# Layer 1 of a fused attention and expert kernel: seven half products for eight on the last 768 tokens of four weight pairs

## Chip, cores and metric

The kernel runs on one NeuronCore of a Trainium2 chip. The metric is the device time of one execution in microseconds (us). Names of engines: PE is TensorE (matmul) and PEld its weight loads, DVE is VectorE, ACT is ScalarE, POOL is GpSimd, SP is the engine that issues most DMAs (SPq in the rows).

## Reference: what is computed

Sigmoid attention over 4 batches, 12 heads, 448 positions of 64, then two layers on the 1792 tokens of 768 features. Layer 1 takes the maximum of three products; its 768x768 weights come as float64 and are converted to float32 on the chip. Layer 2 multiplies by `w_out`; then each token goes to one of 8 experts.

```python
scores = scale * np.matmul(q, k.transpose(0, 1, 3, 2)) - np.log(S)
attn = 1.0 / (1.0 + np.exp(-scores))
x = np.matmul(attn, v)                      # then as (1792, 768)
h = np.maximum(np.maximum(x @ w1, x @ w2), x @ w3)
x = h @ w_out
logits = x @ w_gate + modality_bias[modality_id]
e_idx = np.argmax(logits, axis=1)           # one expert of 8 per token
out[mask] = gate_w[mask, None] * (np.maximum(x[mask] @ w1[e], 0.0) @ w2[e])
```

## The kernel before

Every float32 product is made from two parts of each operand, a rounded high part and the rest (`split`, L184: ACT or DVE writes the high part, DVE the rest), with three matmuls per 128x128 block: high times high, high times low, low times high.

**Stages on PE, in order of time:** attention (L318, L334, L344, L352), layer 1 (`project`, L499), layer 2 in two passes (`layer2`, L563), the experts (L900, L916, L928). PE, DVE, ACT and SP run their instructions in the order in which the code emits them; each engine waits at the head of its queue, and so does SP with its DMAs.

**Layer 1.** Six blocks of 128 output features (`fb`), in each two halves of the tokens (1024, then 768), in each the three weights (`wi`). One call of `project` is a *step* of 36 matmuls: 6 blocks of input features, 3 matmuls each, on two halves of the step's tokens (2x512 or 2x384 columns). It accumulates in one of two PSUM tiles `acc` that take turns. At its end ACT copies the result into `hT` (L503, first weight) or DVE takes the maximum (L505, second and third). `hA` (tag H1) and `hB` (H2) hold all six blocks of h until layer 2.

**Weights.** A *chunk* is one float64 block of 768x128 weights (768 KB) or 128 rows of `w_out`. SP loads it into one of two `stage` buffers, six DVE operations (`cv_ops`, L164) convert it, and `split` puts the parts into one of four places of `w_ring`. All of that, and the products of `w_out` with the gate (`gate_op`, L480, 48 of them), stands in a queue `bg`/`bg2`, from which `background` takes operations after each step until an estimate of their cost is used up (6.6 or 4.8).

**End of layer 1.** While the last steps run, `split_a` and `split_h` make the operands of the first two token tiles of layer 2; `pass_a` then takes the 14 tiles of 128 tokens in order.

Of the kernel before, what the change touches and what calls it, by code (L numbers as in the profile page):

```python
# [23 lines left out]
E64_LO = float(np.uint32(0x38000000).view(np.float32))  # L24
E64_HI = float(np.uint32(0x47EFFFFF).view(np.float32))


@with_exitstack
def attn_moe_kernel(
# [136 lines left out]
    def cv_ops(i, dst):  # L166
# [206 lines left out]
    with tc.manual_schedule(engines={mybir.EngineType.PE, mybir.EngineType.Activation, mybir.EngineType.DVE, SP}):  # L373
# [46 lines left out]
        for j in range(NU // 2 + 1):  # L420
# [48 lines left out]
        gk = hold("K1", "gk", 3 * DM)  # L469
        wgb = [cut(gk, DM * i, DM) for i in range(2)]  # L470
        junk = cut(gk, 2 * DM, DM)

        def gate_load(e):
            for i, (op, cost, at) in enumerate(bg2):
                if at == 1000 + e:
                    bg2[i] = (op, cost, step[0] + 1)
            nc.sync.dma_start(out=wgb[e % 2], in_=wgT[e].partition_broadcast(128))

        def gate_op(e, kb):
            nc.vector.scalar_tensor_tensor(out=junk, in0=wof[kb], scalar=1.0, in1=wgb[e % 2], op0=ALU.mult,  # L480
                                           op1=ALU.mult, accum_out=gw[:, kb, e:e + 1])
# [6 lines left out]

        def project(fb, half, wi):
            while (fb, wi) not in ready:  # L490
                background(0.1, late=0)
            m = w_ring[ring_no[fb, wi]]
            acc = ps_a([128, 2, 512], "acc")
            c0 = HALF * half
            cw = (min(c0 + HALF, NT) - c0) // 2
# [5 lines left out]
            dst = hT[fb][:, c0:c0 + 2 * cw].rearrange("p (c s) -> p c s", c=2)  # L501
            if wi == 0:
                nc.scalar.activation(out=dst, in_=acc[:, :, 0:cw], func=ACTF.Copy)  # L503
            else:
                nc.vector.tensor_tensor(out=dst, in0=dst, in1=acc[:, :, 0:cw], op=ALU.max)  # L505
            if half == 1:
                used[fb, wi] = step[0]

        CA = 256
# [3 lines left out]
        def hs_view(a):  # L515
            return a.rearrange("p (a k c) -> p a k c", a=2, k=KB)

        def split_h(t, hs):
            for h_, k0, k1 in ((hA, 0, 4), (hB, 4, 6)):
                src = h_[:, :, 128 * t:128 * (t + 1)]  # L520
                split(hs[:, 0, k0:k1], hs[:, 1, k0:k1], src)
# [6 lines left out]

        for fb in range(KB):
            for half in range(2):  # L530
                for wi in range(3):
                    project(fb, half, wi)
                    step[0] += 1
                    background(6.6 if half == 0 else 4.8)
                    if fb == KB - 1 and half == 1:

                        assert not bg and not bg2
                        for i in ((0,), (1, 2), ())[wi]:
                            split_a(i)
                        if wi < 2:  # L540
                            hs1[wi] = hs_view(w_ring_[1][:, 0] if wi == 0 else hold("K1", "hs_k", 2 * DM))
                            split_h(wi, hs1[wi])


        wo_ck = hold("P2a", "wo_ck", 2 * KB * DM)
# [24 lines left out]
        def end_a(t):  # L570
            acc = acc_t.pop(t)
            nc.scalar.activation(out=xoa[t % 2], in_=acc[:, 0:CA], func=ACTF.Copy)
            nc.vector.tensor_tensor(out=lg[:, t], in0=bias_t[:, t], in1=acc[:, CA:NA], op=ALU.add)
            nc.sync.dma_start(out=x2d[0][128 * t:128 * (t + 1), 0:CA], in_=xoa[t % 2])

# [448 lines left out]
        def end_b(p, c=None):  # L1024
            rows = slice(128 * toks[p], 128 * (toks[p] + 1))
            a, b = out_b(p, c)
# [8 lines left out]
        def put_gate(p):  # L1035
            b = out_b(p, None if p < P0 else 1)[1]
            nc.vector.tensor_copy(out=b[:, DM - 512:DM - 511], in_=gate[:, toks[p]:toks[p] + 1])

# [221 lines left out]
```

## Time and profile before

| what | value |
|---|---|
| median of 3 runs | 735.28 us (734.99 to 736.02) |
| the profiled execution | 731.45 us, of which the span shown in the trace is 729.6 us |
| PE busy | 721.0 us, 99% of the span |
| DVE, ACT, POOL busy | 486.5, 263.2, 77.0 us |
| layer 1 on PE | 131.74 to 391.53 us |
[...]

Busy PE counts pipelined matmuls, so it says that PE has no pauses, not that it is at its peak. The other engines work beside PE; their time counts only where PE waits for them.

### The profile page before, as it was taken

How to read it: one execution, taken by the hardware profiler on the slowest of the kernel's cores; microseconds unless marked ns; L12 is line 12 of the kernel's file. 1: busy time of each engine (PE TensorE's matmuls, PEld its weight loads, DVE VectorE, ACT ScalarE, POOL GpSimd, SP SyncE). 2: the span in 40 equal slices, each digit the busy share in tenths (PEclk: the TensorE clock that was granted, in tenths of full speed). 3: DMA queues.
4: the chain of work that ended last, by engine and by line, in shares of the span. 5: the costliest groups of instructions: out<-in, count | busy, mean ns of one | idle time of the engine just before them, and what ended most of it. 6: DMA issues, size and time to landing. Idle time of an engine off the chain costs nothing.

```text
span 729.6 us, 10665 instructions
## 1 busy us (share of the span) xinstructions
PE 721.0 (99%) x4164; PEld 613.9 (84%) x4164; DVE 486.5 (67%) x845; ACT 263.2 (36%) x410; POOL 77.0 (11%) x96
## 2 busy tenths in 40 slices
PE   8999999999999999999999999999999999999996
PEld 5455545799898988989899988998998899999996
DVE  4677885666877879873125657146895698689363
ACT  5665566000011010100123533243661474375352
POOL 3000000000000000000001004453025005101101
PEclk9999999999999999999999999999999999999999
DMA  8856761141332321310000113668154025515101
GB/s 204 214 158 167 195 185 54 44 130 54 124 129 91 95 94 44 108 44 1 0 1 22 66 53 126 191 190 308 57 190 158 0 75 174 199 53 193 51 2 63
DMA packets 42330, 78.58 MB, mean 108 GB/s; under 512 B 6201, under 2 KB 28794, under 8 KB 42276
## 3 DMA queue, kind: packets, MB, share of 16 engines
q1 hardware_dynamic: 38420, 66.10, 30.0%
q0 software_dynamic: 3776, 11.63, 4.6%
q8 instruction: 35, 0.57, 0.3%
q14 instruction: 19, 0.16, 0.1%
q10 hardware_dynamic: 80, 0.11, 0.1%
HBM read 69.79 MB, written 11.58 MB: 112 GB/s over the span
## 4 chain that ended last, share of the span: by engine, by line
PE 98%; DMA 0%; SPq 0%; issue 0%; DVE 0%; POOL 0%; POOLq 0%; ACT 0%; ACTq 0%
PE acc L499 36%; PE hacc L900 16%; PE oacc L928 12%; PE X L344 8%; PE s L318 7%; PE acc_b L563 5%; PE acc_a L563 4%; PE oacc L916 3%; PE acc_c L563 3%; PE X L352 2%; PE xT L788 1%; PE s L334 1%; DMA u<-in_qk_dram 0%; SPq L269 0%; PE wgp L360 0%
## 5 line engine op out<-in xcount | busy, mean ns | idle before, releaser
L499 PE MATMUL acc<-xR,w_ring 128*128 128x512 f32 (+1 forms) x864 | 208.3, 362 | 0.0
L499 PEld LDWEIGHTS acc<-xR,w_ring 128*128 128x128 f32 x864 | 157.6, 188 | 17.6 <-issue 0.7
L900 PE MATMUL hacc<-xh,wo_ck 128*128 128x512 f32 (+3 forms) x600 | 120.6, 361 | 0.0
L900 PEld LDWEIGHTS hacc<-xh,wo_ck 128*128 128x128 f32 x600 | 107.1, 188 | 12.1 <-DVE xo L948 0.3
L499 PE MATMUL acc<-xLa,w_ring 128*128 128x512 f32 (+1 forms) x360 | 101.3, 362 | 0.0
L301 ACT ACTIVATE at<-s,nlns 128x896 f32<-128x896 f32 x84 | 77.9, 1007 | 44.4 <-PE s L318 43.0
L928 PE MATMUL oacc<-wo_ck,hx 128*128 128x384 f32 x504 | 90.3, 336 | 0.0
L928 PEld LDWEIGHTS oacc<-wo_ck,hx 128*128 128x128 f32 x504 | 87.2, 188 | 0.2
L189 DVE TENSOR_TENSOR wo_ck<-raw,wo_ck 128x512 fp32r<-128x512 f32 (+1 forms) x87 | 68.4, 807 | 24.6 <-ACT wo_ck L188 24.5
L499 PEld LDWEIGHTS acc<-xLa,w_ring 128*128 128x128 f32 x360 | 66.3, 188 | 7.1
L188 ACT ACTIVATE wo_ck<-raw 128x512 fp32r<-128x512 f32 (+1 forms) x87 | 59.6, 723 | 18.6 <-DVE raw L823 7.6
L318 PEld LDWEIGHTS s<-kq 64*128 64x128 f32 x432 | 37.9, 185 | 21.3 <-issue 15.5
L318 PE MATMUL s<-kq 64*128 64x448 f32 x432 | 50.9, 376 | 0.8 <-ACT kq L287 0.8
L503 ACT ACTIVATE hA<-acc 128x1024 f32<-128x1024 f32 (+1 forms) x8 | 7.4, 922 | 118.3 <-PE acc L499 118.3
L480 DVE SCALAR_TENSOR_TENSOR gk<-wof,gk 128x768 f32<-128x768 f32 x48 | 45.9, 957 | 1.4
L997 POOL MEMSET xo<- 128x544 f32 x5 | 2.6, 550 | 410.6 <-PE acc_a L563 382.1
L775 POOL DMA_INDIRECT xg<-x2d,idx x30 | 36.5, 1218 | 74.1 <-PE xT L788 43.8
L344 PE MATMUL X<-at,u 128*64 128x448 f32 x192 | 37.8, 543 | 0.0
L370 DVE CAST xR<-X 128x448 fp32r<-128x448 f32 x24 | 14.9, 619 | 31.9 <-PE X L352 31.9
L505 DVE TENSOR_TENSOR hB<-hB,acc 128x1024 f32<-128x1024 f32 (+1 forms) x8 | 8.7, 1088 | 39.5 <-PE acc L499 39.4
L188 ACT ACTIVATE w_ring<-cv 128x768 fp32r<-128x768 f32 x14 | 11.8, 842 | 54.7 <-PE acc L499 54.7
L505 DVE TENSOR_TENSOR hA<-hA,acc 128x1024 f32<-128x1024 f32 (+1 forms) x16 | 17.4, 1087 | 20.3 <-PE acc L499 19.9
(260 smaller groups left out, 885.2 us busy)
## 6 DMA issues: line engine op xcount, KB each, us to landing
stage<-in_moe_w_dram SPq DMA_DIRECT2D x18, 768.0 KB, 4.5
raw<-in_moe_w_dram SPq DMA_DIRECT2D x12, 1024.0 KB, 5.7
u<-in_qk_dram SPq DMA_DIRECT2D x46, 224.0 KB, 4.8
raw<-in_moe_w_dram SPq DMA_DIRECT2D x12, 768.0 KB, 4.8
stage<-in_moe_w_out_dram SPq DMA_DIRECT2D x6, 768.0 KB
x2d<-xo SPq DMA_DIRECT2D x28, 128.0 KB, 1.7
gk<-wgT SPq DMA_DIRECT2D x8, 384.0 KB, 5.4
rawb<-in_moe_w_dram SPq DMA_DIRECT2D x4, 768.0 KB, 4.6
```

The source lines that it names most:

```text
L188: nc.scalar.activation(out=r(dR), in_=src, func=ACTF.Copy)
L189: nc.vector.tensor_tensor(out=r(dL), in0=src, in1=dR, op=ALU.subtract)
L301: nc.scalar.activation(out=dst, in_=s[:, :, 0:S], func=ACTF.Sigmoid, scale=qscale, bias=nlns)
L318: nc.tensor.matmul(s[g][:, h, 0:S], r(kt[p, a, 0, 128 * g:128 * (g + 1)]), r(kt[p, x, 1]), start=(n == 0), stop=(n == 2))
L344: nc.tensor.matmul(X_t[u][64 * h:64 * h + 64, 0:S], vt[:, 2 * g + h], at[:, 2 * g + h], start=(g == 0), stop=False)
L480: nc.vector.scalar_tensor_tensor(out=junk, in0=wof[kb], scalar=1.0, in1=wgb[e % 2], op0=ALU.mult, op1=ALU.mult, accum_out=gw[:, kb, e:e + 1])
L499: nc.tensor.matmul(acc[:, c, 0:cw], r(m[:, a, kk, :]), r(x[kk][:, c0 + cw * c:c0 + cw * (c + 1)]), start=(kk == 0 and n == 0), stop=(kk == ...
L505: nc.vector.tensor_tensor(out=dst, in0=dst, in1=acc[:, :, 0:cw], op=ALU.max)
L563: nc.tensor.matmul(acc, r(hs[:, a, kk, :]), r(w(kk, b)), start=(kk == 0 and n == 0), stop=(kk == KB - 1 and n == 2))
L775: d = nc.gpsimd.indirect_dma_start(out=xg[s][:, XC[c][0]:XC[c][1]], out_offset=None, in_=x2d[c], in_offset=bass.IndirectOffsetOnAxis(ap=ix ...
L900: st["mm"] = nc.tensor.matmul(acc[:, f, t0:t1], r(w[a][:, k, 128 * f:128 * (f + 1)]), r(x[:, 2 * c + k, t0:t1]), start=(t0 == 0 and c == 0 ...
L928: nc.tensor.matmul(o[:, s, 0:HC], r(hz[k][:, x, 2 * c + f, 128 * s:128 * (s + 1)]), r(w[a][:, f]), start=(first and c == 0 and f == 0 and ...
```

## The change

Layer 1 is now nine *jobs*: three pairs of feature blocks (`p`), for each the three weights. Jobs 0 to 4 are four `plain` steps as before, with the 768 tokens first (n = 0, 1 for the two blocks), then the 1024 (n = 2, 3). Jobs 5 to 8 compute the last 768 tokens of both blocks together by seven products of half-size operands (`s_block`: A11 B11, S2 T2, A12 B21, S1 T1, S3 T3, A22 T4, S4 B22), each of 9 matmuls of 384 columns, where there were two steps, that is eight such products; then two plain steps (f = 0, 1) of 1024 tokens. Sums of the tokens' operands (T1 to T4) are made once, in jobs 0 and 4; sums of the weights (S1 to S4) for each job.

With it come these:

- Conversion: ACT makes the first operation (`conv_start`), DVE four (`conv_end`) instead of six.
- From chunk 16 on (job 5's weights) all loads go into one `stage` buffer, and the next load is issued behind the conversion's last read; the other buffer (tag S1) holds the sums `sm`.
- The order of the side work is written out (`plan`, `do_tasks`, `hook`). In jobs 5 to 7 one chunk is converted in the last step, one inside `s_block` behind the first product (`hook(0)`).
- H1 holds the T sums, so h of pairs 0 and 1 is written to HBM (`spill`) and read back into `hA` in job 8.
- Layer 2 takes the tokens from 1024 on first (`tok`).

```diff
+    hd = dram.tile([128 * (KB - 2), NT], F32, name="hd")
...
+    def conv_start():
...
+        if k < NC1:
+            load_chunk()
+        v = cv1 if k >= NC1 or k % 2 == 0 else cv2
+        st = stage[k % 2 if k < NC1 else 0]
+        hf = st.bitcast(F32).rearrange("p (n two) -> p n two", two=2)[:, :, 1]
+        nc.scalar.activation(out=v, in_=hf, func=ACTF.Copy, scale=E64_SC)
+        return k, v, st
+
+    def conv_end(c, dsts):
...
+        ve.tensor_scalar(out=v, in0=v, scalar1=-E64_TOP, scalar2=E64_TOP, op0=ALU.max, op1=ALU.min)
+        ve.tensor_scalar(out=v.bitcast(I32), in0=v.bitcast(I32), scalar1=3, scalar2=None, op0=ALU.logical_shift_left)
+        ve.scalar_tensor_tensor(out=v.bitcast(U32), in0=lo.bitcast(U32), scalar=29, in1=v.bitcast(U32),
+                                op0=ALU.logical_shift_right, op1=ALU.bitwise_or)
+        for d, c0, c1 in dsts or [(v, 0, DM)]:
+            ve.scalar_tensor_tensor(out=d.bitcast(U32), in0=hi[:, c0:c1].bitcast(U32), scalar=0x80000000,
+                                    in1=v[:, c0:c1].bitcast(U32), op0=ALU.bitwise_and, op1=ALU.bitwise_or)
+        if k >= NC1:
+            load_chunk()
+        return v
...
-            nc.sync.dma_start(out=stage[i % 2].rearrange("p (a c) -> p a c", a=n), in_=src)
+            nc.sync.dma_start(out=stage[i % 2 if i < NC1 else 0].rearrange("p (a c) -> p a c", a=n), in_=src)
...
+        def s_sums():
+            ve_ = nc.vector.tensor_tensor
+            ve_(out=part(0), in0=raw_b[0], in1=raw_b[1], op=ALU.add)
+            ve_(out=part(1), in0=part(0), in1=raw_a[0], op=ALU.subtract)
+            ve_(out=part(2), in0=raw_a[0], in1=raw_b[0], op=ALU.subtract)
+            ve_(out=part(3), in0=raw_a[1], in1=part(1), op=ALU.subtract)
...
+        def prod(a, b, g, first):
+            a, b = aop(a), bop(b)
+            for kk in range(K2):
+                for n, (i, x) in enumerate(((0, 0), (0, 1), (1, 0))):
+                    nc.tensor.matmul(g[:, 0:SW], r(a(i, kk)), r(b(x, kk)), start=(first and kk == 0 and n == 0),
+                                     stop=(kk == K2 - 1 and n == 2), skip_group_check=not first)
...
+            prod("A11", "B11", g0, True)
+            nc.scalar.activation(out=t1, in_=g0[:, c], func=ACTF.Copy)
+            hook(0)
+            prod("S2", "T2", g1, True)
+            ve_(out=t2, in0=t1, in1=g1[:, c], op=ALU.add)
+            hook(1)
+            prod("A12", "B21", g0, False)
+            take(g0[:, c], hp[:, 0, S0_], wi)
+            hook(2)
+            prod("S1", "T1", g2, True)
+            hook(3)
+            prod("S3", "T3", g1, False)
+            ve_(out=t3, in0=t1, in1=g1[:, c], op=ALU.add)
+            fin(t3, g2, hp[:, 1, S1_])
...
+        plan.update({(FJ - 1, 0): "ca", (FJ - 1, 1): "cb", (FJ - 1, 2): "T3", (FJ - 1, 3): "S cn"})
...
+            split_aw(1)
+            if j == FJ:
+                s_split(1)
+
+            def hook(i):
+                step[0] += 1
+                if i == 0 and not end:
+                    conv_end(conv_start(), DST[1])
+
+            s_block(hp, wi, hook)
...
+            if end:
...
+                hA = hold("H1", "hA", 4, NT)
+                for c in (S0_, S1_, slice(0, HALF // 2), slice(HALF // 2, HALF)):
+                    nc.sync.dma_start(out=hA[:, :, c], in_=hd.rearrange("(k p) n -> p k n", p=128)[:, :, c])
...
+                elif f == 0:
+                    s_sums()
+                    for i in range(2):
+                        s_split(i)
+                    background(2.1)
+                else:
+                    background(2.1)
+                    split_aw(0)
+                    if j < NJOB - 2:
+                        conv_end(conv_start(), DST[0])
+                take(acc, hp[:, f, B0_], wi)
```

On PE, a step of 768 tokens before (one block, one weight) begins like this; its results go to `acc`, and its first matmul waits for the reader of that PSUM tile:

```order
L499 MATMUL acc<-xR,w_ring_78 128x384 [waits DVE_49]
L499 MATMUL acc<-xR,w_ring_78 128x384
L499 MATMUL acc<-xLa,w_ring_78 128x384 x2
L499 MATMUL acc<-xR,w_ring_78 128x384 x4
L499 MATMUL acc<-xLa,w_ring_78 128x384 x2
L499 MATMUL acc<-xR,w_ring_78 128x384 x4
```

In job 5 of the changed kernel, from the second product (S2 T2 into g1, here `g_2232`) to the start of the fifth (S3 T3, into the same g1), PE has this:

```order
L637 MATMUL g_2232<-tT,w_ring_78 128x384 x6
L637 MATMUL g_2231<-xR,w_ring_79 128x384 [waits Activation_49]
L637 MATMUL g_2231<-xLa,w_ring_79 128x384
L637 MATMUL g_2231<-xR,w_ring_79 128x384 x2
L637 MATMUL g_2231<-xLa,w_ring_79 128x384
L637 MATMUL g_2231<-xR,w_ring_79 128x384 x2
L637 MATMUL g_2231<-xLb,w_ring_79 128x384
L637 MATMUL g_2231<-xR,w_ring_79 128x384
L637 MATMUL g_2233<-tT,w_ring_78 128x384 x9
L637 MATMUL g_2232<-xR,w_ring_78 128x384 [waits DVE_49]
```

The fifth product adds to g1, so its first matmul waits for DVE's reading of g1 (`t2`, L657); between the two stand only the third and fourth product.

On DVE, a conversion before stands like this at one of the last steps of layer 1 (`cv` is the converted chunk); it is six operations, and a late one delays only the `take` of a step behind it (L505):

```order
L172 TENSOR_SCALAR cv<-stage_75 128x768
L173 TENSOR_SCALAR cv<-cv 128x768
L174 TENSOR_SCALAR cv<-cv 128x768
L176 SCALAR_TENSOR_TENSOR cv<-stage_75,cv 128x768
L178 TENSOR_SCALAR cv<-stage_75 128x768
L180 TENSOR_TENSOR cv<-cv 128x768
L505 TENSOR_TENSOR hA<-hA,acc 128x768
L189 TENSOR_TENSOR w_ring_79<-cv,w_ring_79 128x768
```

From the last `take` of job 4 into job 5's `s_block`, the changed kernel has this on DVE (`sm` the sums, `h_1845` h of pair 1):

```order
L631 TENSOR_TENSOR h_1845<-h_1845,acc 128x1024
L221 TENSOR_TENSOR w_ring_79<-cv,w_ring_79 128x768
L221 TENSOR_TENSOR w_ring_78<-sm,w_ring_78 128x768
L204 TENSOR_SCALAR cv<-cv 128x768
L205 TENSOR_SCALAR cv<-cv 128x768
L206 SCALAR_TENSOR_TENSOR cv<-stage_75,cv 128x768
L209 SCALAR_TENSOR_TENSOR cv<-stage_75,cv 128x768
L657 TENSOR_TENSOR sm<-sm,g_2232 128x384
L631 TENSOR_TENSOR h_1845<-h_1845,g_2231 128x384
L665 TENSOR_TENSOR sm<-sm,g_2232 128x384
```

A whole conversion (L204 to L209) now stands ahead of the reading of g1 (L657).

On SP, the last loads of layer 1 before take turns between the two buffers (`gk` are the gate's operands):

```order
L223 DMA stage_75<-in_moe_w_dram 128x6x256
L223 DMA stage_76<-in_moe_w_dram 128x6x256
L223 DMA stage_75<-in_moe_w_dram 128x6x256
L477 DMA gk<-wgT 128x768 x3
L223 DMA stage_76<-in_moe_w_dram 128x6x256
L223 DMA stage_75<-in_moe_w_dram 128x6x256
L223 DMA stage_76<-in_moe_w_dram 128x6x256
```

In the changed kernel the loads from job 4 on (chunks 17 to 23) all go into one buffer, with the spills between them and the reading back at the end:

```order
L261 DMA stage_75<-in_moe_w_dram 128x6x256 x4
L677 DMA hd<-h_1845 128x768 x2
L514 DMA gk<-wgT 128x768
L677 DMA hd<-h_1845 128x1024
L261 DMA stage_75<-in_moe_w_dram 128x6x256
L677 DMA hd<-h_1845 128x1024
L261 DMA stage_75<-in_moe_w_dram 128x6x256 x2
L772 DMA hA<-hd 128x4x384 x2
L772 DMA hA<-hd 128x4x512 x2
```

No load of chunks 17 to 23 can be issued ahead of the last reading of the chunk before it.

## Rows read from the trace of the kernel before

**Rows 1.** The page: busy time of the engines, and granted TensorE clock in 40 slices.

```profile
PE 721.0 (99%) x4164; PEld 613.9 (84%) x4164; DVE 486.5 (67%) x845; ACT 263.2 (36%) x410; POOL 77.0 (11%) x96
...
PEclk9999999999999999999999999999999999999999
```

**Rows 2.** Chain that ended last, in order of time: start us, us, what, count.

```profile
131.74 259.79 PE acc L499 x1296
391.53 30.54 PE acc_a L563 x252
...
534.66 4.17 PE oacc L928 x24
```

**Rows 3.** Who waited for whom; total us, times, longest: PE, whole span.

```profile
PE warm L391 <- DVE nlns L379: 1.3, 1, 1.3
PE s L318 <- ACT kq L287: 0.8, 1, 0.8
```

**Rows 4.** Timeline 120 to 160 us: start us, us, engine, line: last part of x.

```profile
133.62 0.62 DVE L371 TENSOR_TENSOR xLb<-X,xR 128x448 fp32r<-128x448 f32 x1
```

**Rows 5.** Groups by shape, VectorE, 131 to 395 us: count, busy us, mean ns, idle before.

```profile
L480 DVE SCALAR_TENSOR_TENSOR gk<-wof,gk 128x768 f32<-128x768 f32 x48 | 45.9, 957 | 1.4
L176 DVE SCALAR_TENSOR_TENSOR cv<-stage,cv 128x768 uint32<-128x768 uint32 x20 | 19.2, 958 | 0.7
...
L173 DVE TENSOR_SCALAR cv<-cv 128x768 f32<-128x768 f32 x20 | 11.2, 561 | 0.7
...
L505 DVE TENSOR_TENSOR hA<-hA,acc 128x1024 f32<-128x1024 f32 x8 | 9.8, 1219 | 5.2 <-PE acc L499 5.2
L505 DVE TENSOR_TENSOR hA<-hA,acc 128x768 f32<-128x768 f32 x8 | 7.6, 955 | 15.0 <-PE acc L499 14.6
...
L480 DVE DVE_READ_ACCUMULATOR gk<-wof,gk 128x1 f32 x48 | 4.0, 82 | 0.0
...
L189 DVE TENSOR_TENSOR wo_a<-wof,wo_a 128x512 fp32r<-128x512 f32 x3 | 2.1, 688 | 6.4 <-ACT wo_a L188 6.4
...
L189 DVE TENSOR_TENSOR hs_p<-hB,hs_p 128x256 fp32r<-128x256 f32 x2 | 0.8, 421 | 0.0
```

**Rows 6.** Groups by shape, ScalarE, whole span.

```profile
L188 ACT ACTIVATE w_ring<-cv 128x768 fp32r<-128x768 f32 x14 | 11.8, 842 | 54.7 <-PE acc L499 54.7
...
L188 ACT ACTIVATE hs_p<-hA 128x512 fp32r<-128x512 f32 x7 | 4.4, 623 | 8.1 <-PE acc L499 8.1
L503 ACT ACTIVATE hA<-acc 128x1024 f32<-128x1024 f32 x4 | 4.1, 1030 | 34.3 <-PE acc L499 34.3
...
L942 ACT ACTIVATE xo<-oacc,gcol 128x384 f32<-128x384 f32 x6 | 3.5, 580 | 0.3
```

**Rows 7.** Timeline 300 to 312 us, one conversion and the next load.

```profile
301.91 0.56 DVE L174 TENSOR_SCALAR cv<-cv 128x768 int32<-128x768 int32 x1
...
302.50 0.96 DVE L176 SCALAR_TENSOR_TENSOR cv<-stage,cv 128x768 uint32<-128x768 uint32 x1
...
303.38 0.56 DVE L178 TENSOR_SCALAR cv<-stage 128x768 uint32<-128x768 uint32 x1
...
303.96 6.57 SPq L223 DMA_DIRECT2D stage<-in_moe_w_dram  x2
```

**Rows 8.** DMA issues: count, KB each, median us from issue to landing.

```profile
stage<-in_moe_w_dram SPq DMA_DIRECT2D x18, 768.0 KB, 4.5
...
x2d<-xo SPq DMA_DIRECT2D x28, 128.0 KB, 1.7
```

**Rows 9.** Tile stage, 260 to 345 us: landing time of its loads.

```profile
DMA to landing us min/median/max: 4.5/5.1/5.6
```

**Rows 10.** Busy us (instructions) of PE, PEld, DVE, ACT, POOL; PEclk; DMA share; GB/s.

```profile
4.00:6.00 2.00, 1.25 (x9) 0.94 (x10) 1.58 (x4) 0.39 (x1) 2.00 (x8) 1.00 0.82 238
304.50:307.50 3.00, 3.00 (x15) 2.53 (x15) 2.85 (x4) 0.85 (x1) 0.00 (x0) 1.00 0.82 247
```

More of the change, by code (lines that the diff above doesn't have):

```diff
@@ L487, in attn_moe_kernel, with xpart @@
                 bg2.extend((lambda e=e - 1, kb=kb: gate_op(e, kb), US_SUM, 1000 + e - 1) for kb in range(KB))
[L489 to L492, printed above, removed]
+        def xpart(x, k, c):
+            if x == 0:
+                return [(slice(0, K2), xR_[:, K2 * k:K2 * (k + 1), c])]
+            if k == 0:
+                return [(slice(0, K2), xLa[:, 0:K2, c])]
+            return [(slice(0, K2 - 1), xLa[:, K2:KB - 1, c]), (slice(K2 - 1, K2), xLb[:, :, c])]
@@ new lines, in minus_plus, with step_, t_prep @@
+        def minus_plus(d, first, rest):
+            def step_(a, b, op):
+                for sl, ap in b:
+                    nc.vector.tensor_tensor(out=d[:, sl], in0=a[:, sl], in1=ap, op=op)
+            ops = [lambda: step_(*first, ALU.subtract)]
+            ops += [lambda p=p, op=op: step_(d, p, op) for op, p in rest]
+            return ops
+        US_T = 1.35
+        ADD, SUB = ALU.add, ALU.subtract
+        def t_prep():
+            tt = hold("K1", "tt", 2, K2, SW)
+            tA, tB = tt[:, 0], tt[:, 1]
+            whole = lambda a: [(slice(0, K2), a)]
+            ops = minus_plus(tA, (xpart(0, 0, S1_)[0][1], xpart(0, 0, S0_)), [(SUB, xpart(1, 0, S0_)), (ADD, xpart(1, 0, S1_))])
+            ops.append(lambda: split(tT[:, 0, 0], tT[:, 0, 1], tA))
+            ops += minus_plus(tB, (xpart(0, 1, S1_)[0][1], whole(tA)), [(ADD, xpart(1, 1, S1_))])
+            ops.append(lambda: split(tT[:, 1, 0], tT[:, 1, 1], tB))
+            ops += minus_plus(tA, (xpart(0, 1, S0_)[0][1], whole(tB)), [(ADD, xpart(1, 1, S0_))])
+            ops.append(lambda: split(tT[:, 2, 0], tT[:, 2, 1], tA))
+            return ops
@@ L493, in project, with s_split, split_aw, plain @@
+        def s_split(i):
+            m = sw_[i]
+            split(flat(m[:, 0]), flat(m[:, 1]), cut(sm_[0], 2 * QW * i, 2 * QW))
+        def split_aw(f):
+            if f:
+                split(flat(aw[1][:, 0]), flat(aw[1][:, 1]), cv2)
+                return
+            for k, src in enumerate(raw_a):
+                split(ksl(aw[0], 0, k), ksl(aw[0], 1, k), src)
+        def plain(m, c0, n_tok):
             acc = ps_a([128, 2, 512], "acc")
-            c0 = HALF * half
-            cw = (min(c0 + HALF, NT) - c0) // 2
+            cw = n_tok // 2
@@ L504, in project @@
             else:
[L505 to L507 removed]
+                nc.vector.tensor_tensor(out=dst, in0=dst, in1=acc, op=ALU.max)
+        def prod(a, b, g, first):
[4 more added lines that the diff above has]
+                                     stop=(kk == K2 - 1 and n == 2), skip_group_check=not first)
@@ new lines, in s_block, with fin @@
+        def s_block(hp, wi, hook):
+            g0, g1 = (ps(f"x{i}", [128, 512], f"g{i}") for i in range(2))
+            g2 = ps("t", [128, 2, 512], "g2")[:, 0]
+            t1, t2, t3, t4 = (part(i) for i in range(4))
+            c = slice(0, SW)
+            ve_ = nc.vector.tensor_tensor
+            def fin(u, g, dst):
+                d = dst if wi == 0 else t4
+                ve_(out=d, in0=u, in1=g[:, c], op=ALU.add)
+                if wi:
+                    ve_(out=dst, in0=dst, in1=t4, op=ALU.max)
+            prod("A11", "B11", g0, True)
[12 more added lines that the diff above has]
+            fin(t3, g2, hp[:, 1, S1_])
+            hook(4)
+            g3 = ps("x0", [128, 512], "g3")
+            prod("A22", "T4", g3, True)
+            fin(t3, g3, hp[:, 1, S0_])
+            hook(5)
+            prod("S4", "B22", g2, False)
+            fin(t2, g2, hp[:, 0, S1_])
+            hook(6)
@@ L511, in attn_moe_kernel, with spill @@
+        def spill(p, hp, f, c):
+            nc.sync.dma_start(out=hd[128 * (2 * p + f):128 * (2 * p + f + 1), c], in_=hp[:, f, c])
+        B0_, B1_ = slice(0, HALF), slice(HALF, NT)
         CA = 256
@@ L527, in split_a @@
             split(w[:, :, 0, CA:NA], w[:, :, 1, CA:NA], gw[:, 2 * i:2 * i + 2, 0:E])
[L529 to L532, printed above, removed]
-                    step[0] += 1
[L534 to L542, printed above, removed]
+        tq = deque(t_prep())
@@ L1024, in end_b @@
         def end_b(p, c=None):
-            rows = slice(128 * toks[p], 128 * (toks[p] + 1))
+            rows = slice(128 * tok[toks[p]], 128 * (tok[toks[p]] + 1))
             a, b = out_b(p, c)
```

175 lines of the change are left out of this document (142 added, 33 removed).

## Prediction

> **What bounds the kernel now.** I read the page first: PE is busy for 99% of the span, at a granted clock in the highest tenth in every slice [rows 1]. The chain that ended last is PE from one end to the other, layer 1 as one piece of 259.79 us with 1296 matmuls [rows 2]. The waits say the same: after its first instruction PE waited once, 0.8 us, and never in layer 1 [rows 3]. So PE's own work sets the time. Whatever takes matmuls away is worth their length, and whatever makes PE wait costs its whole length, since no slack lies behind. DVE and ACT have time to spare over the whole, but they work in a fixed order, and where PE needs a reading of theirs, their place in that order decides.
>
> **The gain.** 24 matmuls of 384 columns take 4.17 us [rows 2], so 0.174 us each. Layer 1 has 648 of those, 112.6 us; the other 648, of 512 columns, take the remaining 147.2, so 0.227 each. A step of 36 is then 6.26 or 8.18 us, a job of four steps 28.88, a half product of nine 1.56 and a block of seven 10.95 in place of 12.51. Four blocks save 4 x 1.56 = **6.26 us**. That the nine now write one PSUM tile without a turn costs nothing by the rows: `pass_a` does that and takes 30.54/252 = 0.121 us for 264 columns [rows 2], in proportion to the columns as 0.174 is.
>
> [...]
>
> **The prices of side work.** On DVE [rows 5]: a two-operand pass over 768 elements 0.96 us, over 512 0.69, over 256 0.42, so by these an estimate of 0.55 for 384 and 1.35 for 1152; the maximum of a step (`take`) 1.22 or 0.96; a gate product 0.96 + 0.08, which I take as 1.0. A one-operand pass is 0.56, and a dependent one follows after 0.60 [rows 7]. On ACT [rows 6]: 0.84 for 768, 0.62 for 512, 1.03 for a `take` of 1024, 0.58 for 384 from PSUM. The new conversion is then 0.84 on ACT, then 0.60 + 0.60 + 0.99 + 0.96 = 3.15 on DVE (3.2 where its last pass is in two halves). A load is issued 0.02 us after the last reading of its buffer [rows 7] and lands 4.5 us later in the median [rows 8]; in the late stretch of layer 1 it was 4.5 to 5.6 [rows 9]. No row has an ACT pass over every second element, which the conversion now begins with; I take the price of a plain one.
>
> **The new wait.** In each block the fifth product adds to g1, which DVE has to read first (`t2`, 0.55). PE reaches it after four products, 6.26 us into the block. In jobs 5, 6 and 7 a whole conversion stands ahead of `t2` on DVE, and its chunk is loaded only after the conversion before it has ended, because one buffer serves all. Both are followed here; handing over costs about 0.05 each time.
>
> *Job 5.* From job 4's start: ACT's `take` of job 3 and its conversion, 1.95; DVE 3.2, at 5.15 the load of chunk 17 goes out; landed 9.65, ACT 0.85, DVE 3.15, at 13.7. A gate product and a `take`, 15.6. T3: passes over 1152, 1152, 768 and 384, 4.2, then ACT 1.2 and DVE 1.4 for its parts, 22.4. Gate and `take`, 24.6 (PE ended that step at 20.7, so DVE is what is late). Four sums 2.1 and a split 0.9, 27.6. The conversion of chunk 18, 3.2, at 30.8: only now is chunk 19 loaded, and PE began the block at 28.88. Landing 4.5, ACT 0.85, DVE 3.15, `t2` 0.55 and the handing over 0.15 make 40.0, which is 11.1 into the block: **4.8 us of pause**.
>
> *Job 6.* From the end of job 5's first plain step: `take` 1.22, two gate products 2.0, two half splits 1.0, conversion 3.2, so the load goes out at 7.45, 0.7 before the block (the step in between is 8.18). Landed 3.8 into it; 4.65 more for ACT, DVE, `t2` and handing over, 8.45: **2.2 us**.
>
> *Job 7.* Here ACT makes the `take`s: 1.03, two copies 1.0, conversion 0.85, DVE 3.2 make 6.1, so the load goes out 2.1 before the block, lands at 2.4, and 4.65 more give 7.05: **0.8 us**. Job 8 has no conversion in its block: `take` 1.22 and a split 1.0 end before the second product does, no pause.
>
> Together **7.8 us**. With 5.6 us for each load (job 5 has two in its chain) they would be 12.2; with 4.4 and DVE's passes 5% shorter, 5.6.
>
> **What I cost at nothing, and its cover.**
> - The sums T1, T2, T4 (ten tasks in job 0) and the late start of DVE's work there: ACT makes job 0's `take`s, so DVE may run into job 1. By the same prices DVE is about 6 us behind when job 1 begins, and its `take` of that job's first step ends at 12.2 into the job, when PE is about to reuse that PSUM tile at 12.5. That cover is thin, 0.3 us; beyond it each us counts.
> - The first step now reads the last tokens of attention. DVE has written them by 134.24 us [rows 4], 2.5 us into layer 1; PE needs the fifth block of features at 24 x 0.174 = 4.2.
> - The spills (384 and 512 KB, after a `take`): nearest rows 128 KB in 1.7 us and 768 KB in 4.5 [rows 8], so between these. h of the next pair is written at the earliest 6.26 us after the last one's `take` began; on SP they stand ahead of loads, but are issued before those loads could be. If not hidden: up to 1 us each.
> - The reading back, 3.67 MB, goes out when the sixth product of job 8 has ended, 9.4 into its block. At 247 GB/s, measured while a load ran [rows 10], it lasts 15 us and ends at about 26.5. The first quarter, some 3 us and the landing time, is needed at 20; the last part from 33 on. Seven us of cover.
> - Handing over between products: no row has PE waiting on a semaphore that was given long before; 0 to 0.1 for each, I take 0.
>
> **The sum.** Against the profiled execution: 731.45 - 6.26 + 7.8 = 733.0. The median of the runs lies 3.83 above that execution (735.28), so I add the difference to it: 735.28 + 1.5 = **736.8 us**. What PE saves on products it loses at the fifth product of three blocks, to a load that starts too late. With the bounds above this case reaches from 734.6 to 741.2; I expect 735 to 739.
>
> **Rivals.**
>
> *The loads arrive in time (faster).* If DVE gets through job 4 faster than my sum, chunk 19 goes out earlier, and every us there is a us less pause. For: 27 passes and two loads stand in that chain, and an error adds up; the order leaves DVE free to run ahead. Against: DVE waits 2.3 us for chunk 17 whatever happens, and 4.8 us would be a sixth of its chain. With no pause in any job: 735.28 - 6.26 = 729.0; with half of them 732.9. It is faster by over 0.2% if the pauses make less than 4.8 together. Chance 0.19.
>
> *The clock falls (slower).* PE would stand still for 4.8 us in job 5. [...] It decides only if the pause is there at all. Chance 0.15.
> [...]
>
> *Something I cost at nothing is late (slower).* Most likely the first `take`s of job 1, or the spills and the reading back where they meet loads: 1 to 4 us on top, 738 to 741. The point is 0.3 us of delay in job 1, or the reading back at half its rate. Chance 0.08.
>
> **How the numbers follow.** The forecast has 0.58, at 736.8. Below 733.8 or above 736.75 a time differs from 735.28 by over 0.2%, about what a measurement of this kernel can tell from no change. Of the forecast's 0.58 some 0.23 lie within that; with 0.01 of the first rival that makes *same* 0.24. *Faster* is the rest of the first rival, 0.18. *Slower* is 0.35 + 0.15 + 0.08 = 0.58. For 8 in 10 the range runs from 731.5, which leaves out two thirds of the first rival, to 740.5, which leaves out the worst of the last two.
>
> **What would show it.** In the changed kernel's waits, PE should wait for DVE `sm` at L657 three times, about 4.8, 2.2 and 0.8 us, at the first matmul of S3 T3, and ACT's conversion just before for the load of `stage`. Layer 1 on PE should last about 261 us with 1260 matmuls. The granted clock after the longest pause tells the second rival. The forecast is wrong if those waits are short (then DVE's chain in job 4 is where to look), if half products are slower than 0.174 us a matmul, or if `pass_a` waits for `hA`.

## Result, and the profile after

| | median | before, same chip | ratio, 95% interval |
|---|---|---|---|
| the changed kernel | 739.03 us (736.15 to 741.59, 8 runs) | 735.08 us | 1.0052 (1.0027 to 1.0077) |
| again (e5) | 736.47 us (735.27 to 739.00, 10 runs) | 734.66 us | 1.0032 (1.0020 to 1.0044) |

It is slower, by 2 to 4 us. The forecast was 736.8, the range 731.5 to 740.5, and the rival in which the clock falls had a chance of 0.15. The profiled execution of the first row took 741.45 us, its span is 739.6; it is next to the longest of the eight.

The page of the changed kernel, the rows that answer to [rows 1]: PE is busy for 98% of the span, and one slice of the granted clock is below the highest tenth (its mean is 0.992, in the kernel before 0.999).

```profile
PE 722.7 (98%) x4128; PEld 613.2 (83%) x4128; DVE 511.4 (69%) x880; ACT 293.7 (40%) x449; POOL 77.3 (10%) x96
...
PEclk9999999999999998999999999999999999999999
```

The chain that ended last (start us, us, what, count) answers to [rows 2]. Layer 1 on PE goes from 134.49 to 399.33 us, 264.84 where it was 259.79; the forecast was about 261. The lines of 27 matmuls are what follows a wait in a block, products five to seven.

```profile
134.49 115.68 PE acc L621 x576
...
289.39 7.11 PE g L637 x27
...
320.91 6.54 PE g L637 x27
...
350.65 4.98 PE g L637 x27
...
372.00 10.97 PE g L637 x63
...
399.33 30.52 PE acc_a L816 x252
```

In the block of job 8, where nothing waits, 63 matmuls take 10.97 us (10.95 expected); so 27 take 4.70. Behind the three waits they took 7.11, 6.54 and 4.98. Behind the last the granted clock was 1.00 (350.65 to 355.63 us), so its 0.28 us more is not the clock's; below it is called the restart.

Who waited for whom (total us, times, longest), PE, whole span, answers to [rows 3]:

```profile
PE g L637 <- DVE sm L657: 6.5, 3, 4.1
PE acc_c L816 <- issue: 1.5, 2, 0.8
...
PE s L351 <- DVE kq L321: 0.9, 1, 0.9
```

The first line is the wait that was forecast. The chain to it in job 5 (start us, us, engine, line; in brackets the idle time before and what ended it):

```profile
278.86 0.33 PE L637 MATMUL g<-xR,w_ring 128*128 128x384 f32 x1
...
279.30 1.03 DVE L209 SCALAR_TENSOR_TENSOR wof<-stage,cv 128x384 uint32<-128x384 uint32 x2
...
280.24 1.21 DVE L631 TENSOR_TENSOR h<-h,acc 128x1024 f32<-128x1024 f32 x1
...
280.40 8.92 SPq L261 DMA_DIRECT2D stage<-in_moe_w_dram  x2
...
284.81 0.89 ACT L195 ACTIVATE cv<-stage 128x768 f32<-128x768 f32 x1 [3.67 <-DMA stage<-in_moe_w_dram]
285.73 0.56 DVE L204 TENSOR_SCALAR cv<-cv 128x768 f32<-128x768 f32 x1 [2.54 <-ACT cv L195]
...
287.92 0.96 DVE L209 SCALAR_TENSOR_TENSOR cv<-stage,cv 128x768 uint32<-128x768 uint32 x1
288.79 0.55 DVE L657 TENSOR_TENSOR sm<-sm,g 128x384 f32<-128x384 f32 x1
...
289.39 0.69 PE L637 MATMUL g<-xR,w_ring 128*128 128x384 f32 x1 [4.10 <-DVE sm L657]
```

The load of chunk 19 goes out at 280.40, when the conversion of chunk 18 has ended, 1.54 us after the first product of the block began (278.86). 4.4 us later ACT begins, then DVE's four passes, then `t2`, then PE, which had waited 4.10 us. The rows of jobs 6 and 7:

```profile
320.91 0.44 PE L637 MATMUL g<-xR,w_ring 128*128 128x384 f32 x1 [1.78 <-DVE sm L657]
...
350.65 0.45 PE L637 MATMUL g<-xR,w_ring 128*128 128x384 f32 x1 [0.57 <-DVE sm L657]
```

The stretches around the waits of jobs 5 and 6 (PE, PEld, DVE, ACT, POOL busy us with instructions, then PEclk, DMA share, GB/s) answer to [rows 10]:

```profile
283.00:285.00 2.00, 2.00 (x14) 1.97 (x12) 0.19 (x1) 0.19 (x1) 0.00 (x0) 1.00 0.54 192
...
287.00:289.40 2.40, 0.01 (x1) 0.01 (x1) 2.37 (x4) 0.00 (x0) 0.00 (x0) 0.55 0.00 0
289.40:291.00 1.60, 1.60 (x5) 1.60 (x6) 0.40 (x1) 0.00 (x0) 0.00 (x0) 0.50 0.33 112
...
293.50:294.60 1.10, 1.10 (x7) 1.10 (x6) 0.88 (x2) 0.00 (x0) 0.00 (x0) 0.74 0.00 0
294.60:295.00 0.40, 0.40 (x4) 0.40 (x3) 0.05 (x1) 0.00 (x0) 0.00 (x0) 1.00 0.00 0
...
318.00:320.90 2.90, 1.13 (x7) 0.81 (x5) 2.79 (x4) 0.10 (x1) 0.00 (x0) 1.00 0.00 0
320.90:322.00 1.10, 1.09 (x5) 1.09 (x6) 0.00 (x0) 0.00 (x0) 0.00 (x0) 0.72 0.20 47
322.00:324.00 2.00, 2.00 (x8) 2.00 (x7) 0.18 (x1) 0.00 (x0) 0.00 (x0) 0.50 1.03 357
```

While PE stands in job 5, the granted clock falls: its mean is 0.55 from 287.00 to 289.40; while PE works again it is 0.50 up to 293.50, 0.74 from there to 294.60, and then 1.00. In job 6 it was still 1.00 up to 320.90, while PE stood, and was at 0.50 only from 322.00 to 324.00, when PE worked again.

So layer 1 is accounted for: 253.82 without any wait (measured below), 6.45 of waiting and 4.53 of slower products behind the waits make 264.80.

Outside of layer 1 this execution was 4.9 us longer than the rows of before: 2.75 ahead of it (the first 18 products of the program began 0.8 us later and took 3.73 us, before 2.09) and 2.15 in the last pass of layer 2 (L816, 1.5 of it the waits for `issue` above). Neither comes with the change as such: of the 13 other traces one has that slow start (e6), and the `issue` waits stand in all four that were taken on one chip (e5 to e8) and in none of the eight of e1 to e4 and e9 to e12. Whether the kernel before has such waits on that chip is not shown, as it was not traced there.

### The profile page after: what moved, and what is told of

The parts are those of the page before. It is cut to its first block, busy times and chain, and to the rows that moved or that the text cites. A ratio compares the mean times of both kernels' runs of the same rounds, so it can differ in the third digit from the quotient of the medians.

```text
span 739.6 us, 10728 instructions
## 1 busy us (share of the span) xinstructions
PE 722.7 (98%) x4128; PEld 613.2 (83%) x4128; DVE 511.4 (69%) x880; ACT 293.7 (40%) x449; POOL 77.3 (10%) x96
## 4 chain that ended last, share of the span: by engine, by line
PE 89%; DVE 6%; DMA 2%; ACT 1%; issue 1%; SPq 0%; POOL 0%; POOLq 0%; ACTq 0%; DVEq 0%
PE acc L621 23%; PE hacc L1153 16%; PE oacc L1181 12%; PE X L377 8%; PE s L351 7%; PE acc_b L816 5%; PE acc_a L816 4%; PE g L637 4%; PE oacc L1169 3%; PE acc_c L816 3%; DMA stage<-in_moe_w_dram 2%; PE X L385 1%; PE s L367 1%; PE xT L1041 1%; DVE cv L206 1%
## 5 line engine op out<-in xcount | busy, mean ns | idle before, releaser
L621 PE MATMUL acc<-xR,w_ring 128*128 128x512 f32 (+1 forms) x672 | 168.0, 370 | 0.0
L621 PEld LDWEIGHTS acc<-xR,w_ring 128*128 128x128 f32 x672 | 123.5, 188 | 17.4 <-issue 0.7
L221 DVE TENSOR_TENSOR wo_ck<-raw,wo_ck 128x512 fp32r<-128x512 f32 (+1 forms) x87 | 68.3, 807 | 28.0 <-ACT wo_ck L220 24.8
L621 PE MATMUL acc<-xLa,w_ring 128*128 128x512 f32 (+1 forms) x280 | 80.9, 370 | 0.0
L621 PEld LDWEIGHTS acc<-xLa,w_ring 128*128 128x128 f32 x280 | 51.8, 188 | 7.2
L351 PE MATMUL s<-kq 64*128 64x448 f32 x432 | 52.5, 386 | 0.9 <-DVE kq L321 0.9
L637 PE MATMUL g<-xR,w_ring 128*128 128x384 f32 x96 | 29.4, 361 | 6.5 <-DVE sm L657 6.5
L220 ACT ACTIVATE w_ring<-cv 128x768 fp32r<-128x768 f32 x10 | 8.4, 844 | 60.8 <-DVE cv L209 46.4
L377 PEld LDWEIGHTS X<-at,u 128*64 128x64 f32 x192 | 13.1, 137 | 21.0 <-issue 17.0
L1226 POOL DMA_INDIRECT out_dram<-xo,idx x15 | 16.1, 1072 | 96.1 <-DVE xo L1201 49.4
```

The lines of the kernel that those rows point to most:

```text
L351: nc.tensor.matmul(s[g][:, h, 0:S], r(kt[p, a, 0, 128 * g:128 * (g + 1)]), r(kt[p, x, 1]), start=(n == 0), stop=(n == 2))
L377: nc.tensor.matmul(X_t[u][64 * h:64 * h + 64, 0:S], vt[:, 2 * g + h], at[:, 2 * g + h], start=(g == 0), stop=False)
L637: nc.tensor.matmul(g[:, 0:SW], r(a(i, kk)), r(b(x, kk)), start=(first and kk == 0 and n == 0), stop=(kk == K2 - 1 and n == 2), skip_group_ ...
```

## Experiments

Each of three sets has its own runs of the kernel before: 731.67 us beside e1 to e4, 731.65 beside e9 to e12 on the same chip, 734.66 beside e5 to e8 on another. So ratios are compared, and layer 1 by its length on PE in the trace.

| run | median us | ratio to before | layer 1 us | PE's waits in it, us |
|---|---|---|---|---|
| e1 | 726.04 | 0.9925 (0.9911 to 0.9938) | 253.82 | none |
| e2 | 732.09 | 1.0007 (0.9998 to 1.0016) | 260.09 | none |
| e3 | 732.49 | 1.0013 (1.0003 to 1.0022) | 260.31 | 3.88, 0.43 |
| e4 | 732.28 | 1.0012 (1.0003 to 1.0021) | 260.50 | 3.97 |
| e5 | 736.47 | 1.0032 (1.0020 to 1.0044) | 263.28 | 3.99, 1.66, 0.52 |
| e6 | 732.46, one run | | 256.84 | 1.43, 0.33, 0.39 |
| e7 | 730.84 | 0.9946 (0.9929 to 0.9962) | 257.05 | 1.41, 0.95 |
| e8 | 727.59 | 0.9901 (0.9884 to 0.9917) | 254.11 | 1.44 |
| e9 | 731.42, one run | | 259.79 | none |
| e10 | 732.76, one run | | 260.77 | 2.20, 1.89, 0.4 |
| e11 | 724.50 | 0.9901 (0.9887 to 0.9915) | 252.41 | none |
| e12 | 724.64 | 0.9905 (0.9891 to 0.9919) | 252.73 | 0.64, 0.65 |

**The whole loss undone (e1).** One number moves the conversion in the blocks of jobs 5 to 7 from behind the first to behind the sixth product:

```diff
             def hook(i):
                 step[0] += 1
-                if i == 0 and not end:
+                if i == 5 and not end:
                     conv_end(conv_start(), DST[1])
```

> The conversion inside the blocks of jobs 5 to 7 stands behind the sixth product (hook 5) instead of the first; nothing else differs. In the changed kernel PE waited 4.10, 1.78 and 0.57 us for t2 (L657), and the 81 matmuls behind these three waits took 18.63 us for 3 x 4.70, 4.5 more, at a granted clock of 0.50 after the first two. Theory (the place of the conversion on DVE is the whole loss): no wait of PE at L657, granted clock 1.00 through layer 1, layer 1 on PE 253.5 us where it was 264.8, and the median 735.1 - 6.3 = 728.8 us, ratio to the kernel before 0.991. Rival 1 (the wait moves: the conversion now ends about 15 us into a block, and the next chunk or the sums behind it become late): a new PE wait at the next block or plain step, 732 to 735. Rival 2 (spills, reading back and the new order of side work cost time outside the waits): no wait at L657, but 731 to 733 with layer 1 still near 253.5.

Measured: 726.04 us, 5.63 below the kernel before. PE's waits of the whole execution (who waited for whom) are down to the one of its first instruction:

```profile
PE warm L424 <- DVE nlns L412: 1.3, 1, 1.3
```

The chain has the blocks at full pace:

```profile
132.04 144.53 PE acc L621 x720
276.57 10.96 PE g L637 x63
...
303.89 10.96 PE g L637 x63
```

Layer 1 is 11.02 us shorter than in the changed kernel. The place of the conversion is the loss, and rival 1 fell. The next thing that is close shows in the timeline of SP and ACT, at the start of job 6:

```profile
305.58 0.32 SPq L677 DMA_DIRECT2D hd<-h  x1
...
310.73 0.49 ACT L629 ACTIVATE hB<-g 128x384 f32<-128x384 f32 x1 [4.72 <-DMA hd<-h]
```

ACT's copy of g0 into the new `hB` waits 4.72 us for the last spill, which reads the same buffer. It ends at 311.2; PE needs g0's tile at 311.7 (7.8 into the block). The cover is 0.5 us.

**The price of all the rest (e2).** e1 with the eighth product put back:

```diff
+            prod("A12", "B21", g2, True)
             prod("S1", "T1", g2, True)
```

> As the run before (conversion behind the sixth product), with an eighth half product put back into each of the four blocks: A12 B21 is computed once more into the PSUM tile that the fourth product then overwrites, so the output is the same and PE has the matmuls of the kernel before. Theory: 4 x 1.56 = 6.26 us more than the run before, 735.1, the time of the kernel before: spills, reading back, the first tokens last, the fixed order and the sums then cost nothing. Rival 2 (they cost time): 737 to 739. Rival 3 (a half product is worth less than nine matmuls at 0.174 us): less than 5 us more than the run before.

Measured: 6.05 us more than e1, 0.42 more than the kernel before; the interval reaches from -0.1 to 1.2 us. Its block in job 5, in the chain:

```profile
276.21 12.53 PE g L637 x72
```

12.53 for 10.96: a half product is worth 1.57 us, as reckoned. Spills, reading back, sums and the order by hand cost together what can't be told from nothing (layer 1 is 0.30 us longer than before). Rivals 2 and 3 fell.

**Job 5 alone, jobs 6 and 7 alone (e3, e4).**

```diff
-                if i == 0 and not end:
+                if i == (5 if j == FJ else 0) and not end:
...
-                if i == 0 and not end:
+                if i == (0 if j == FJ else 5) and not end:
```

> The conversion stands behind the sixth product in job 5 alone; jobs 6 and 7 are as in the changed kernel. Theory: the wait of 4.10 us and the 2.4 us at half clock behind it go, those of job 6 (1.78 + 1.84) and job 7 (0.57 + 0.28) stay: 739.0 - 6.5 = 732.5 us. Rival (the block of job 6 is late because of what happens in job 5): its wait goes too, 729 to 730, or grows, 734 and more.

> The conversion stands behind the sixth product in jobs 6 and 7 alone; job 5 is as in the changed kernel. Theory: one wait of 4.1 us with 2.4 us at half clock behind it is left: 739.0 - 4.5 = 734.5 us, and 728.8 + 6.5 = 735.3 counted from the other side. Rival (the pauses alone cost, the clock would have fallen anyway): the loss behind job 5 is the same, but a granted clock under 1.00 is seen in jobs 6 and 7 as well.

Measured against e1: 6.45 us more and 6.24 more; expected were 4.5 (the rest of jobs 6 and 7) and 6.5. e4 is as expected (behind its wait the granted clock was 0.50 from 286.4 to 290), and its rival fell: jobs 6 and 7 took 10.97 us each, the full pace. That e3's median is the 732.5 of its theory is luck, since the kernel before takes 3.4 us less on this chip. In e3 the wait of job 6 grew (timeline of PE):

```profile
314.45 0.44 PE L637 MATMUL g<-xR,w_ring 128*128 128x384 f32 x1 [3.88 <-DVE sm L657]
```

The stretches around it, with columns as above:

```profile
312.00:314.40 2.40, 0.00 (x0) 0.00 (x0) 2.36 (x3) 0.00 (x0) 0.00 (x0) 1.00 0.00 0
314.40:317.00 2.60, 2.55 (x11) 2.56 (x12) 0.37 (x1) 0.00 (x0) 0.00 (x0) 0.77 0.67 225
317.00:319.00 2.00, 2.00 (x8) 2.00 (x8) 0.74 (x2) 0.00 (x0) 0.00 (x0) 0.50 0.33 113
```

3.88 us where it had been 1.78. The load that job 6 waits for goes out in the changed kernel at

```profile
311.96 0.38 SPq L261 DMA_DIRECT2D stage<-in_moe_w_dram  x1
```

and in e3 at

```profile
304.89 0.38 SPq L261 DMA_DIRECT2D stage<-in_moe_w_dram  x1
```

The block of job 6 begins at 312.70 and at 304.14, so the load is 0.74 us ahead of it in the one and 0.75 behind it in the other. That is 1.5 of the 2.1 us; the other 0.6 is that ACT began 4.98 us behind the load instead of 4.37. So the parts don't add up: in the changed kernel the 6.5 us lost in job 5 let DVE catch up before job 6 (in job 5's first plain step DVE there waits 1.22 us for PE, in e3 it does not). The last part of the rival was the true one. In e3 the clock falls only after PE has begun to work again (1.00 up to 314.40, 0.50 from 317.00), and PE loses 1.6 us by it: the 27 matmuls take 6.54 us, where behind a wait they take 4.98 at a granted clock of 1.00.

**The changed kernel once more (e5).** No edit.

> The changed kernel itself, unaltered, beside the kernel before on the same chip. In the first runs its ratio to the kernel before was 1.0052, while its layer 1 was longer by 5.05 us and 4.9 us more stood outside of layer 1 in the profiled execution (2.75 before it, 2.15 in the last pass of layer 2). Theory (only layer 1 differs): layer 1 again 264 to 265 us, three waits of PE at L657 of about 4.1, 1.8 and 0.6 us, and the rest of the execution as long as in the kernel before: 11.0 us more than with the conversion behind the sixth product, ratio near 1.007. Rival (the reading back or the other order of tokens lengthens layer 2): the last pass of layer 2 is again longer by 2 us, ratio 1.009 and more.

The waits are the same, 3.99, 1.66 and 0.52. The products behind them are not (chain):

```profile
286.33 7.41 PE g L637 x27
...
318.03 4.98 PE g L637 x27
...
346.17 4.98 PE g L637 x27
```

This time the clock fell in job 5 alone: it was 0.50 from 286.3 to 290, and 1.00 from 317 to 323, around the wait of job 6; behind that of job 7 the 4.98 us show no fall. It is why layer 1 is 1.6 us shorter than in the first trace, and it fits that the changed kernel's times spread over 3.7 and 5.4 us, those of e1 over 0.8. The ratio is below what I gave: layer 1 is 3.5 us longer than the 259.79 of the two traces of the kernel before, the median only 1.81. The same is seen in e7 and e8: on this chip the difference of the medians is 1.1 to 1.7 us better than that of layer 1, while on the other the two agree within 0.4 in e1 to e4, e11 and e12. Where the kernel before loses that time is not shown, since it was not traced on this chip.

**Late load or place on DVE (e6).** The changed kernel without the loads of the three chunks that are converted inside blocks:

```diff
-            nc.sync.dma_start(out=stage[i % 2 if i < NC1 else 0].rearrange("p (a c) -> p a c", a=n), in_=src)
+            if i < NC1 + 2 or i % 2 == 0:
+                nc.sync.dma_start(out=stage[i % 2 if i < NC1 else 0].rearrange("p (a c) -> p a c", a=n), in_=src)
```

> The changed kernel without the loads of chunks 19, 21 and 23, which are the ones converted inside the blocks of jobs 5 to 7; the conversions run where they stand, on what the buffer holds, so the second feature block of jobs 6 to 8 gets wrong weights. It tells the late load from the place on DVE. Worked out from the changed kernel's trace: in job 5 DVE is busy with the take and two splits until 4.5 us into the block, then conversion 3.15 and t2 0.55: PE waits 1.7 us instead of 4.1. In job 6 the same work ends before PE arrives: no wait instead of 1.78. In job 7 the load had landed when ACT was ready: the wait stays, 0.4 to 0.6. Sum 2.3 instead of 6.45. Theory A (the load is late): as these. Theory B (the place on DVE alone decides): the three waits stay near 4.1, 1.8 and 0.6.

The timeline of PE has three waits (its line numbers are higher by one):

```profile
286.49 0.44 PE L638 MATMUL g<-xR,w_ring 128*128 128x384 f32 x1 [1.43 <-DVE sm L658]
...
314.44 0.44 PE L638 MATMUL g<-xR,w_ring 128*128 128x384 f32 x1 [0.33 <-DVE sm L658]
...
342.47 0.44 PE L638 MATMUL g<-xR,w_ring 128*128 128x384 f32 x1 [0.39 <-DVE sm L658]
```

2.15 us of waiting instead of 6.45, about as theory A had it (1.7, 0, 0.5). Some two thirds of the waiting were the late load, the rest the four passes ahead of `t2`.

**A wait elsewhere (e7).** As e1 with `i == 2`.

> The conversion stands behind the third product (hook 2), so ahead of t3 and of the sum that frees g2 (L649) and behind t2. In job 5 the load lands 6.1 us into the block, conversion, t3 and the first sum end at about 11.3; PE comes to the seventh product, which adds to g2, at 9.4: one wait of 2.0 us at L637 for L649. In jobs 6 and 7 the same chain ends before 9.4: no wait. It tells whether a wait of 2 us in another place brings the clock down as well: granted 0.50 and 1 to 2 us more on the 9 + 27 matmuls behind it (10.96 + 2.0 + 1.5 for the block), 3.5 us more than with the conversion behind the sixth product; without a fall of the clock 2.0 to 2.3 more.

PE waits 1.41 us in job 5 (2.0 expected, the load landed earlier than reckoned) and 0.95 in job 6, where none was expected; the granted clock stays at 1.00 (284 to 289 and 312 to 318 us) and the nine matmuls behind each take 1.85 and 1.84 us for 1.57. The waits in the timeline of PE:

```profile
287.16 0.44 PE L637 MATMUL g<-xR,w_ring 128*128 128x384 f32 x1 [1.41 <-DVE sm L649]
...
315.71 0.44 PE L637 MATMUL g<-xR,w_ring 128*128 128x384 f32 x1 [0.95 <-DVE hB L649]
```

Layer 1 is 3.23 longer than in e1: 2.36 of waits and 0.27 for each of three restarts (in job 7 no wait shows). By the medians it is 1.5 us (the two ratios), each with an interval of about 1.2 us to both sides; the two runs are on different chips, see e5.

**DVE late in job 4 (e10).** The changed kernel with

```diff
-            if (j, n) >= (1, 3):
+            if (j, n) >= (1, 3) and j != 4:
                 background(left)
```

> The changed kernel without the gate products that stand between the steps of job 4 (three; they follow later). The prediction said that DVE is late through job 4 and so sends the load of chunk 19 late. From the changed kernel's trace: the products at 263.60 and 272.12 stand on the chain to that load, 1.0 us each, the one at 256.30 beside the waiting for chunk 17. Theory: the load goes out 2.0 us earlier, the wait in job 5 is 2.1 us instead of 4.1, those of jobs 6 and 7 stay at about 1.8 and 0.5. Rival (the chain hangs on PE's steps, not on DVE): the wait stays near 4.1.

The wait of job 5 is 2.20 us (2.1 expected): what stands on DVE in job 4 sends the load late. The products behind the waits of jobs 5 and 6, in the chain, and the stretches around them:

```profile
285.06 4.99 PE g L637 x27
...
314.56 6.54 PE g L637 x27
```

```profile
285.00:286.50 1.50, 1.44 (x8) 1.44 (x9) 0.47 (x2) 0.00 (x0) 0.00 (x0) 1.00 0.42 107
...
315.50:317.00 1.50, 1.50 (x7) 1.50 (x6) 0.00 (x0) 0.00 (x0) 0.00 (x0) 0.50 0.96 310
```

The clock does not fall behind 2.20 us of waiting (1.00 from 282.8 to 290), and falls to 0.50 behind 1.89.

**The kernel before (e9).** No edit.

> The kernel before, unaltered, for its trace. The rows of before come from an execution of 731.45 us, 3.8 below the median of its runs, and every trace of the changed kernel with a long last pass of layer 2 had PE waiting there for nothing that the profile shows (issue, 0.6 to 1.5 us). Theory: where the median of the kernel before is about 735, its trace shows such waits in the last pass of layer 2 too, so they are not the change's; layer 1 is 259.8 us as in the rows. Rival (the change brings them): none there, and the 3.8 us stand elsewhere.

These runs were on the chip where the kernel before takes 731.65, so the question stays open: no trace of it was taken where the median is 735. What it shows: an execution of 731.42 with layer 1 of 259.79, as in the rows of before. So those rows are most likely from such a chip, and the 3.83 us that I added are a difference between chips more than between executions.

**More blocks (e8, e11, e12).** e1 with `FJ` 4 in place of 5 and `background(3.3)` for the two `background(2.1)` of the plain steps:

> The conversion behind the sixth product, and seven products already from job 4 on (five blocks instead of four; T3 and the first sums move to job 3), with three gate products for each later plain step instead of two so that they don't pile up at the end. Theory (a block is worth 1.57 us as long as DVE and the loads keep up; DVE was busy 12 to 24 of 27 us in a job): 1.57 us less than with four blocks, ratio to the kernel before 0.9903. Rival (DVE is now late in job 3 or 4, where sums, T3 and three conversions stand together): a wait of PE in the block of job 4, 1 to 4 us, ratio 0.993 to 0.997.

The ratio is 0.9901, but layer 1 is longer than in e1, with a wait of 1.44 us for the thin cover of e1: the third gate product per step holds DVE's last maximum, and so the spill. SP and ACT in the timeline of e8:

```profile
306.02 0.32 SPq L677 DMA_DIRECT2D hd<-h  x1
...
311.07 0.49 ACT L629 ACTIVATE hB<-g 128x384 f32<-128x384 f32 x1 [6.61 <-DMA hd<-h]
```

e11 takes that back where `wi == 2`: `background(2.1 if wi == 2 else 3.3)`.

> As the run with five jobs, but with two gate products instead of three for the plain steps where DVE makes the maximum last (wi = 2, job 5). There PE waited 1.4 us in job 6 for ACT's copy of g0 (L629), which waited for the spill of h: it goes out behind DVE's last maximum of job 5, 3.7 us into the block, where it was 1.7 with the conversion moved and four jobs, and ACT's copy has to wait for it to end. Theory: the spill goes out 2 us earlier in the block, no wait is left in layer 1, layer 1 on PE is 252.3 us, and the time 1.4 to 1.8 us less than that run, ratio to the kernel before 0.988. Rival (spill and load share the DMA engines, so the spill lands as late): the wait stays above 1 us, ratio 0.990.

No wait is left and layer 1 is 252.41 us, 1.41 below e1 and 7.38 below the kernel before; the median is 7.15 below it, and 1.54 below e1's, what a fifth block should bring. The ratio stayed at 0.9901 instead of 0.988; e8's came from the other chip. **This is the best version**, 724.50 us where the kernel before takes 731.65; e12 can't be told from it.

e12 has `FJ` 3 and 4.2 for 3.3:

> As the run before with seven products already from job 3 on (six blocks): T3, the first sums and three conversions then stand in job 2, together with DVE's maxima, and later plain steps take four gate products (two where wi = 2). Theory (a block is worth 1.57 us): 1.57 us less than with five, ratio 0.986. Rival (DVE can't do job 2's work in time: by the prices of the trace it has three conversions 9.6, T3 5.6, sums and two splits 4.8, four maxima 4.3, a split 1.0 and two gate products 2.0, 27.3 us of the job's 28.9, and waits for loads come on top): a wait of 2 to 5 us at the block of job 3, slower than with five.

The sixth block brings nothing: PE waits 0.6 us at the start of two blocks (jobs 5 and 8, not job 3 as the rival said) for a split of weights on DVE (L221), and layer 1 is 1.9 us longer than six blocks should make it.

## Why the prediction held, and where it missed

- **What bounds it, and the gain:** right. A block took 10.97 us (10.95), an eighth product 1.57 (1.56); for the four, e2's blocks minus e1's give 6.27 (6.26).
- **The place of the wait, and its cause:** right. PE waits for `t2` in jobs 5, 6 and 7. The chain in job 4 came out close: the load of chunk 17 5.14 us into it (5.15), that of chunk 19 1.54 into the block (1.9).
- **The size of the waits:** 4.10, 1.78 and 0.57 for 4.8, 2.2 and 0.8, 1.35 too much in all. In job 5 PE went on 10.53 us into the block (11.1), so DVE and the load were 0.6 quicker than reckoned; and the wait is counted from the shown end of the fourth product, 6.43 into the block, not from the 6.26 at which the next could have begun. That second part is no gain: each wait costs 0.27 to 0.3 on top of what the view shows, by the 4.98 us that 27 matmuls take behind one at a granted clock of 1.00. I had 0.15 for handing over and nothing for the restart.
- **The clock: the step that failed.** I gave the clock's fall 0.15. No row of before shows a fall or what it costs: the one pause of PE after its first instruction, 0.8 us at a granted clock of 1.00 [rows 3, 10], says nothing about 4 us; so the 0.15, and the upper end of the range as far as it takes the fall in, were my estimate alone. In the runs it fell to 0.50 behind all four waits near 4 us (4.10, 3.99, 3.97, 3.88) and took 1.6 to 2.4 us beyond the restart. In the first trace it fell in job 6 as well (1.56). So the forecast, pauses of that length at full clock, had too much with 0.58. Layer 1 of that trace was 3.5 us longer than the sum: 3.7 more for the clock, 0.8 for three restarts, 0.3 for the rest, 1.35 less for the waits.
- **Luck in the numbers:** the same kernel that took 739.03 took 736.47 in e5, next to the forecast's 736.8, but with the clock falling once, three restarts and shorter waits. A median alone can't tell a case with a fall from one without here; the waits and the granted clock in the traces do.
- **Edits at no cost:** right, by e2. Job 1's first maximum on DVE ended 0.8 us before PE reached that PSUM tile (0.3 reckoned). The reading back went out 9.4 us into the block of job 8, as reckoned; ACT waited 0.4 us for it, PE never. The spills I had at up to 1 us; e8 shows that they are the next to be late, 1.44.
- **"The loads arrive in time":** 729.0 was its time on the base of 735.28. e1 is 0.9925 x 735.28 = 729.8.
- **The base:** the 3.83 us between rows and median were carried over rightly; by e9 they are most likely a difference between chips, not between executions.

## What to carry to other kernels

When PE has to wait for a reading in the middle of a block, look at what stands ahead of that reading on its engine and what that in turn waits for; a whole conversion, fed by a buffer that is only free when the last conversion is done, belongs behind the last reading that PE needs. A wait of PE cost more here than it shows, a restart of 0.27 to 0.3 us each time and 1.6 to 2.4 us more where the granted clock fell to 0.50, so that a pause of 4 us was worth 5.7 to 6.7. And before adding up the parts of a fix, ask whether one stall had given another engine the time to catch up (e3).

## Unexpected in the hardware

- **The clock's fall did not go by the wait's length alone.** It fell behind waits of 1.78 and 1.89 us and not behind 2.20 and 1.66, in the same kernel behind 1.78 in one execution and not behind 1.66 in another; by an estimate from the means, if it went from 1.00 to 0.50 at once, it fell in e3 some 1.3 us after PE had begun again (a mean of 0.77 over 2.6 us), in job 6 of the first trace some 0.5 us after (0.72 over 1.1). What decides is not settled here.
- **A slow start that the granted clock doesn't show.** In the first trace and in e6, 18 products at the start of the program took 3.73 us, elsewhere 2.09 to 2.62; in the first trace the granted clock was 1.00 in that stretch (6 to 12 us). Cause open.
- ACT's pass over every second element (`conv_start`) took 0.87 to 0.93 us in the first trace, 0.90 in the median; a plain one of 768 took 0.84. The stride costs 0.06 us here.
